# Attention and a mixture of experts on one core: keys and queries loaded head dimension first, the softmax division moved onto x, a column-tiled gate, and longer runs of one tiling

## The chip, the core and the metric

The kernel is one launch on one NeuronCore of a Trainium2 chip. The metric is device time in microseconds (us), the median of several runs; a profiled execution gives the trace that is read here. The engines are named as in the profile: PE (TensorE; PEld is its weight load), DVE (VectorE), ACT (ScalarE), POOL (GpSimd) and SP (SyncE, which here only starts transfers).

## The reference

All data are float32. Attention has 4 batches, 8 heads, 1152 positions and a head dimension of 64; queries are averaged in pairs first, so that 576 are left. Its output becomes x with 2304 rows of 512, which goes through a mixture of 8 experts whose weights P come from eight rounds of row and column scaling (Sinkhorn).

```python
q_pool = q.reshape(B, H, S // 2, 2, D).mean(axis=3)
scores = scale * np.matmul(q_pool, k.transpose(0, 1, 3, 2))
attn = np.exp(scores - scores.max(-1, keepdims=True))
attn = attn / (attn.sum(-1, keepdims=True) + 1e-09)
x = np.matmul(attn, v)                     # to (B*S/2, H*D)
P = np.exp(x @ w_gate - (x @ w_gate).max())
for _ in range(8):
    P /= P.sum(1, keepdims=True) + 1e-09
    P /= P.sum(0, keepdims=True) + 1e-09
    P *= N / E
for e in range(E):
    out += P[:, e:e + 1] * (np.maximum(x @ w1[e], 0.0) @ w2[e])
```

## The kernel before, in words

The program has two stages, attention and then the mixture of experts.

**Attention** goes over 16 pairs of heads (4 batches, 4 pairs). A pair has five units: four full ones, each with 128 queries of both heads, and a mixed one with the last 64 queries of each head. In a unit:

- the scores S are three groups of 384 keys (`qk`, L465). Queries and keys are each split in a high and a low part, so a group takes three products per head. A full unit runs its two heads on two row tiles of the array, 64 rows each; the mixed unit uses the whole array;
- DVE copies S from PSUM to E and keeps the row maximum (`out_max`, L472), ACT takes the exponential in place with its row sum (`expo`, L488), DVE makes the reciprocal of the sum (`rec`, L494 and L495), and ACT or DVE multiplies E by it (`norm`, L503 or L505, 1152 columns at a time);
- PE transposes E, 18 blocks of 128x128 in a full unit and 9 in the mixed one (`tr`, L521), in groups of four that share a PSUM buffer; ACT or DVE copies each group to ET (`tr_out`, L531 or L533);
- PE multiplies ET with the values (`av`, L549), two heads on two column tiles of 64. When a pair's four full units are done, ACT copies the sum to x (`x_out`, L566).

Before a pair starts, its queries and keys are loaded in rows (L378 to L382), POOL adds the two queries of each average (`q_add`, L399 and L402), PE transposes queries and keys (`trans`, L423), ACT writes the high part from PSUM (`hi`, L428) and DVE the low part (`lo`, L436).

The gate's logits are products of 128 rows of x, as weights of the array, with the gate matrix of 8 columns (`gate`, L62). Those of row blocks 0 to 12 run inside attention, the last five at the start of the second stage.

The order of attention is made when the program is built: a planner (`Plan.order`, from L200) keeps for each engine the work that is ready, takes the one of the lowest due time, and places it with a cost in ns. `STICK` is what a PE step gains in due time for having the tiling of the step before; `gap` is the cost of a change of tiling, `WAIT` how long an engine may stay idle for a better step. `CAPS` are the buffers: 2 for S, 3 for transposes, 1 for `av`, 4 for E, 2 for ET. The engines then run their instructions in exactly that order.

**The mixture of experts** (`moe`) is 96 steps of matrix products with split operands: 4032 products of 384 columns (L692 to L694) and 3456 of 512 columns (L729). Here the framework's scheduler sets the order. The Sinkhorn rounds are worked off in small pieces between the steps.

## Time and profile before

| | |
|---|---|
| time, median of 3 runs | 2059.75 us (2058.86 to 2060.17) |
| span of the profiled execution, first to last instruction | 2055.5 us |
| its own time beside the span | not given apart; the median of the runs lies 4.25 us above the span |
| PE busy | 2035.5 us (99%), 13344 instructions |
| PEld busy | 1802.2 us (88%) |
| DVE busy | 1522.8 us (74%) |
| ACT busy | 972.0 us (47%) |
| POOL busy | 336.2 us (16%) |
| granted PE clock, mean of the span | 0.998 |
| DMA | 191952 packets, 135.90 MB, mean 66 GB/s |

A matmul's row gives its start and how long it lay in the array; the next one starts before it ends. What a matmul costs in a stream is therefore read from start to start, not from its duration. A float32 product of x, E or v shows as two matmul records. Attention's products end at 542.4 us, the rest of the gate follows, and the mixture of experts starts at 546.95 us: the first stage is a good quarter of the span.

### The profile page before, as it was taken

Reading aid. Unit: us, or ns where it says so; the run is one execution under the profiler, and the core shown is the slowest. Engines: PE = TensorE matmul, PEld = TensorE weight load, DVE = VectorE, ACT = ScalarE, POOL = GpSimd, SP = SyncE. Lnnn points to the kernel's source line nnn. Section 1 sums busy time; section 2 is a strip of 40 time slices with the busy share of each in tenths; the row PEclk is TensorE's granted clock in tenths of the full one; section 3 lists DMA queues with packets and bytes.
Section 4 is the critical chain, followed back from the end, with each engine's and each line's share of the span. In section 5 each row is a group of like instructions: output and inputs, shape, how many; then the busy total and the mean of one; then the engine's idle time right before and its main releaser. Section 6 shows DMA issues by size and latency. Waiting matters only on the chain.

```text
span 2055.5 us, 33894 instructions
## 1 busy us (share of the span) xinstructions
PE 2035.5 (99%) x13344; PEld 1802.2 (88%) x13344; DVE 1522.8 (74%) x3254; ACT 972.0 (47%) x1617; POOL 336.2 (16%) x424
## 2 busy tenths in 40 slices
PE   8999999999999999999999999999999999999999
PEld 6888888888989999999989999999989999999998
DVE  6787878877698676776776776767776777777764
ACT  6888887888643333233344333333333333333331
POOL 1000011100001112112231211121122112112210
PEclk9999999999999999999999999999999999999999
DMA  5212121210122222222231221222213222222211
GB/s 137 59 48 71 53 54 46 61 47 13 32 82 84 61 83 62 62 73 72 62 103 58 77 70 54 82 62 62 77 47 113 72 65 69 72 59 75 70 54 41
DMA packets 191952, 135.90 MB, mean 66 GB/s; under 512 B 44080, under 2 KB 160816, under 8 KB 191792
## 3 DMA queue, kind: packets, MB, share of 16 engines
q1 hardware_dynamic: 189456, 133.15, 22.3%
q8 instruction: 104, 1.70, 0.4%
q10 hardware_dynamic: 2336, 0.59, 0.1%
q14 instruction: 56, 0.46, 0.1%
HBM read 128.99 MB, written 4.72 MB: 65 GB/s over the span
## 4 chain that ended last, share of the span: by engine, by line
PE 94%; ACT 3%; DVE 2%; DMA 1%; issue 0%; POOL 0%; SPq 0%; ACTq 0%; DVEq 0%
PE pso L729 38%; PE psh L692 11%; PE psh L694 11%; PE psh L693 11%; PE av L549 7%; PE tr L521 7%; PE S L465 6%; PE tr L423 2%; ACT E L488 1%; ACT E L503 1%; ACT ET L531 1%; PE tr L62 1%; DVE xcl L95 0%; DMA qr<-in_q_dram 0%; DVE E L472 0%
## 5 line engine op out<-in xcount | busy, mean ns | idle before, releaser
L701 ACT ACTIVATE hh<-c 128x384 fp32r<-128x384 f32 x384 | 199.9, 521 | 676.0 <-DVE c L712 675.8
L729 PE MATMUL pso<-w2h,hl 128*128 128x512 f32 x1152 | 453.8, 394 | 0.4 <-DVE hl L702 0.4
L692 PE MATMUL psh<-xch,w1h 128*128 128x384 f32 x1344 | 453.0, 337 | 0.7 <-ACT p L707 0.7
L694 PE MATMUL psh<-xch,w1l 128*128 128x384 f32 x1344 | 453.1, 337 | 0.0
L729 PE MATMUL pso<-w2l,hh 128*128 128x512 f32 x1152 | 452.9, 393 | 0.0
L693 PE MATMUL psh<-xcl,w1h 128*128 128x384 f32 x1344 | 451.8, 336 | 0.0
L729 PE MATMUL pso<-w2h,hh 128*128 128x512 f32 x1152 | 447.8, 389 | 0.0
L739 DVE SCALAR_TENSOR_TENSOR x<-pso,PR,x 128x512 f32<-128x512 f32 x264 | 197.4, 748 | 195.6 <-PE pso L729 195.3
L692 PEld LDWEIGHTS psh<-xch,w1h 128*128 128x128 f32 x1344 | 253.0, 188 | 12.7 <-ACT p L707 1.7
L693 PEld LDWEIGHTS psh<-xcl,w1h 128*128 128x128 f32 x1344 | 252.7, 188 | 11.0
L129 POOL TENSOR_TENSOR w1t<-w1s 128x256 f32<-128x256 f32 x88 | 80.9, 920 | 1087.5 <-DMA w1s<-in_moe_w_dram 638.2
L729 PEld LDWEIGHTS pso<-w2h,hl 128*128 128x128 f32 x1152 | 216.0, 188 | 46.2 <-DVE hl L702 0.8
L472 DVE TENSOR_SCALAR_CACHE_REDUCE E<-S 128x384 f32<-128x384 f32 x432 | 222.7, 553 | 43.6 <-PE S L465 41.7
L694 PEld LDWEIGHTS psh<-xch,w1l 128*128 128x128 f32 x1344 | 252.7, 188 | 0.1
L729 PEld LDWEIGHTS pso<-w2l,hh 128*128 128x128 f32 x1152 | 216.1, 188 | 40.0
L729 PEld LDWEIGHTS pso<-w2h,hh 128*128 128x128 f32 x1152 | 216.5, 188 | 38.7
L702 DVE SCALAR_TENSOR_TENSOR hl<-c,hh 128x384 fp32r<-128x384 f32 x384 | 225.2, 587 | 12.2 <-ACT hh L701 0.4
L712 DVE TENSOR_TENSOR c<-psh,u 128x384 f32<-128x384 f32 x288 | 151.2, 552 | 54.4 <-PE psh L694 53.3
L488 ACT ACTIVATE E<-E,st 128x1152 f32<-128x1152 f32 x144 | 179.5, 1252 | 7.0 <-DVE st L478 6.0
L521 PE MATMUL tr<-ident,E 128*128 128x128 f32 x1296 | 172.2, 278 | 4.7 <-ACT ET L531 1.3
L465 PE MATMUL S<-kT,qT 64*128 64x384 f32 (+1 forms) x1296 | 171.7, 362 | 1.3 <-DVE E L472 1.3
L521 PEld LDWEIGHTS tr<-ident,E 128*128 128x128 f32 x1296 | 141.4, 141 | 27.9 <-issue 11.6
(83 smaller groups left out, 2332.5 us busy)
## 6 DMA issues: line engine op xcount, KB each, us to landing
w1s<-in_moe_w_dram SPq DMA_DIRECT2D x192, 256.0 KB, 3.2
w2s<-in_moe_w_dram SPq DMA_DIRECT2D x96, 512.0 KB, 3.6
vt<-in_v_dram SPq DMA_DIRECT2D x16, 576.0 KB, 4.1
kr<-in_k_dram SPq DMA_DIRECT2D x30, 288.0 KB, 4.4
qr<-in_q_dram SPq DMA_DIRECT2D x32, 256.0 KB, 4.3
out_dram<-x SPq DMA_DIRECT2D x18, 256.0 KB, 2.1
qr<-in_q_dram SPq DMA_DIRECT2D x32, 32.0 KB, 4.0
kr<-in_k_dram ACTq DMA_DIRECT2D x2, 288.0 KB, 5.5
```

The source lines that it names most:

```text
L465: nc.tensor.matmul(ps[:, h, :PK], D["qT", p][rows, x, t * P:(t + 1) * P], D["kT", p][rows, y, j * PK:(j + 1) * PK], start=(i == 0), stop=( ...
L472: nc.vector.tensor_scalar(out=D["E", m][:, h, j * PK:(j + 1) * PK], in0=D["sc", m, j][:, h, :PK], scalar1=1.0, scalar2=None, op0=ALU.mult, ...
L488: nc.scalar.activation(out=x, in_=x, func=ACTF.Exp, bias=D["st", m][:, h, 3:4], accum_out=D["rs", p][:, t, h:h + 1])
L521: nc.tensor.transpose(ps[:, i * P:(i + 1) * P], x[:, c * P:(c + 1) * P], ident)
L692: nc.tensor.matmul(ps, hi[:, a, c, :], xch[:, b, c, :], start=(c == 0), stop=False)
L693: nc.tensor.matmul(ps, hi[:, a, c, :], xcl[:, b, c, :], start=False, stop=False)
L694: nc.tensor.matmul(ps, lo[:, a, c, :], xch[:, b, c, :], start=False, stop=(c == 1))
L701: nc.scalar.activation(out=hh[:, fh, ts], in_=src, func=ACTF.Relu)
L702: nc.vector.scalar_tensor_tensor(out=hl[:, fh, ts], in0=src, scalar=0.0, in1=hh[:, fh, ts].bitcast(F32), op0=ALU.max, op1=ALU.subtract)
L712: nc.vector.tensor_tensor(out=y, in0=ps, in1=t, op=ALU.add)
L729: nc.tensor.matmul(ps, u[:, fh, ms], w[:, fh, :], start=(n == 0), stop=(n == 11))
L739: nc.vector.scalar_tensor_tensor(out=a, in0=ps, scalar=PR[:, m, e:e + 1], in1=a, op0=ALU.mult, op1=ALU.add)
```

## The change: what it does

1. **Inputs are laid out before the launch.** A new function `laid_out` reorders the arrays in memory: queries and keys with the head dimension first, values and expert weights so that one transfer loads a tile with long rows per partition. It does no arithmetic. The gate matrix is padded from 8 to 32 columns with zeros.
2. **No input transposes.** `trans` is gone. ACT writes the high part of queries and keys straight from the loaded tile (`q_hi`, `k_hi`), and POOL the low part (`q_lo`, `k_lo`; DVE for the first pair). The factor 0.0625 moves from the queries into `out_max`.
3. **Division on x.** `norm` is gone; the transposes take E right after the exponential. The row sums of a pair's nine heads-by-units lie in one tile; one `rec` per pair adds 1e-9 and inverts. Four small transfers write the 1152 reciprocals to DRAM (`spread_out`), two read them back spread over 64 partitions each (`spread_in`), and POOL multiplies x by them (`x_scale`). What reads x (the gate, the blocks of x for the second stage) now waits for `x_scale`.
4. **Column-tiled gate.** The gate matrix, 32 columns wide, is the weight; x streams 384 columns through, four column tiles at a time; an ACT copy, three transposes and a DVE copy put the logits in place. The last six row blocks follow in the second stage (`last_gate`), after its first step, and the Sinkhorn rounds start there.
5. **The planner's numbers.** `STICK` 0.7 becomes 6.0, `WAIT` 700 becomes 300, the cost of a change of tiling 110 or 60 becomes 195 or 145, `TR0` 12 becomes 14, and the mixed unit's scores count as the same tiling as transposes.

```diff
-        wg = const.tile([P, ND, E], F32, name="wg")
+        wg = const.tile([P, ND, 32], F32, name="wg")
...
-def gate(nc, ps, x, wg, m):
-
-    g, i = divmod(m, MT)
-    for c in range(ND):
-        nc.tensor.matmul(ps, x[:, g, c, i * P:(i + 1) * P], wg[:, c, :], start=(c == 0), stop=(c == ND - 1))
...
+def gate(nc, ps, x, wg, c, chunks, w, t0):
+
+    for j in chunks:
+        g, u = divmod(t0 + j * w, TG)
+        nc.tensor.matmul(ps[32 * j:32 * j + 32, :w], wg[:, c, :], x[:, g, c, u:u + w], start=(c == 0), stop=(c == ND - 1))
...
         t = self.raw1[k] = self.stage.tile([P, 2, ND, P], F32, name="w1s", tag="w1s")
-        for h in range(2):
-            f0 = h * F // 2 + i * P
-            self.nc.sync.dma_start(out=t[:, h], in_=self.w1[e, :, f0:f0 + P].rearrange("(c p) f -> p c f", p=P))
+        self.nc.sync.dma_start(out=t, in_=self.w1[k % (E * FQ)].rearrange("p (h c f) -> p h c f", h=2, c=ND))
...
-    WAIT = 700
+    WAIT = 300
...
-                        gap = 110 if "R2" in (mode, o["mode"]) else 60
+                        gap = 195 if o["mode"] == "R" else 145
...
-TR0 = 12.0
-STICK = 0.7
-CAPS = dict(kr=2, qr=2, vt=2, qa=2, kT=2, qT=2, S=2, tr=3, av=1, E=4, ET=2, st=4, rs=2, avs=2)
-UNIT, MIXED = 5.0, 3.2
+TR0 = 14.0
+STICK = 6.0
+CAPS = dict(kr=2, qr=2, vt=2, qa=2, kT=2, qT=2, S=2, tr=3, av=1, E=4, ET=2, st=4, rs=2, RB=2, lg=1)
+UNIT, MIXED = 6.0, 3.0
...
-        @op("SP", 1800, T - 16, w=[("raw", p)], new=[(("kr", p), "kr"), (("qr", p), "qr")], lat=2500)
-        def load():
-            kr = D["kr", p] = sbt([P, NC, 2, HD], F32, "kr")
-            qr = D["qr", p] = sbt([P, 2 * QT + 1, 2, HD], F32, "qr")
...
+        @op("SP", 1200, T - 16, w=[("q", p)], new=[(("qr", p), "qr")], lat=2500)
+        def load_q():
+            qr = D["qr", p] = sbt([P, 2, Q], F32, "qr")
+            nc.sync.dma_start(out=qr, in_=q[p])
...
-                    nc.tensor.transpose(ps[:, j * P:(j + 1) * P], x, ident)
...
-                nc.scalar.activation(out=D[tag, p][:, 0, c0 * P:(c0 + n) * P], in_=D["ps", p, i][:, :n * P],
-                                     func=ACTF.Copy, scale=0.0625 if what == "q" else 1.0)
...
-                nc.vector.scalar_tensor_tensor(out=t[:, 1, cs], in0=ps, scalar=0.0625 if what == "q" else 1.0,
-                                               in1=t[:, 0, cs].bitcast(F32), op0=ALU.mult, op1=ALU.subtract)
...
+            def q_hi(cs=cs):
+                nc.scalar.activation(out=qT()[:, 0, cs], in_=D["qa", p][:, cs], func=ACTF.Copy)
+
+            @op(ae, cost(ae, n, two=True), T + 5 + 4 * i, r=[("qh", p, i)], w=[("qT", p, i)], use=[("qa", p), ("qT", p)])
+            def q_lo(cs=cs):
+                t = D["qT", p]
+                eng_of[ae].tensor_tensor(out=t[:, 1, cs], in0=D["qa", p][:, cs], in1=t[:, 0, cs].bitcast(F32), op=ALU.subtract)
...
+            def k_hi(cs=cs):
+                nc.scalar.activation(out=kT()[:, 0, cs], in_=D["kr", p][:, cs], func=ACTF.Copy)
+
+            @op(ae, cost(ae, W, two=True), T + 7 + 0.5 * j, r=[("kh", p, j)], w=[("kT", p, j)], use=[("kr", p), ("kT", p)])
+            def k_lo(cs=cs):
+                t = D["kT", p]
+                eng_of[ae].tensor_tensor(out=t[:, 1, cs], in0=D["kr", p][:, cs], in1=t[:, 0, cs].bitcast(F32), op=ALU.subtract)
...
-                    nc.vector.tensor_scalar(out=D["E", m][:, h, j * PK:(j + 1) * PK], in0=D["sc", m, j][:, h, :PK], scalar1=1.0,
+                    nc.vector.tensor_scalar(out=D["E", m][:, h, j * PK:(j + 1) * PK], in0=D["sc", m, j][:, h, :PK], scalar1=0.0625,
...
-        @op("DVE", 260, T + 5.6 + 1.3 * (nt - 1), r=[("X", m, h) for h in heads], w=[("r", m)], use=[("rs", p)])
-        def rec():
-            y = D["rs", p][:, t, :nt]
-            nc.vector.tensor_scalar(out=y, in0=y, scalar1=1e-9, scalar2=None, op0=ALU.add)
-            nc.vector.reciprocal(y, y)
-
-        for h in heads:
-            @op(("DVE", "ACT"), [870, 1053], T + 5.8 + 1.3 * (nt - 1) + 0.1 * h, r=[("r", m)], w=[("E", m, h)], use=[("rs", p), ("E", m)])
-            def norm(eng, h=h):
-                y = D["E", m][:, h]
-                z = D["rs", p][:, t, h:h + 1]
-                if eng == "ACT":
-                    nc.scalar.activation(out=y, in_=y, func=ACTF.Copy, scale=z)
-                else:
-                    nc.vector.tensor_scalar(out=y, in0=y, scalar1=z, scalar2=None, op0=ALU.mult)
...
-            es = [("E", m, h) for h in sorted({c // NC for c in cs})]
+            es = [("X", m, h) for h in sorted({c // NC for c in cs})]
...
+        if mixed:
+            @op("DVE", 260, T + 8, r=[("X", p * (QT + 1) + i, h) for i in range(QT + 1) for h in (range(2) if i < QT else (0,))],
+                w=[("r", p)], use=[("rs", p)])
+            def rec():
+                y = D["rs", p]
+                nc.vector.tensor_scalar(out=y, in0=y, scalar1=1e-9, scalar2=None, op0=ALU.add)
+                nc.vector.reciprocal(y, y)
+
+            @op("SP", 1200, T + 8.2, r=[("r", p)], w=[("rd", p)], use=[("rs", p)], lat=2500)
+            def spread_out():
+                s, y = D["rd", p] = dr.tile([2, Q], F32, name="rd", tag="rd", bufs=2), D["rs", p]
+                for h in range(2):
+                    nc.sync.dma_start(out=s[h, :QM].rearrange("(t p) -> p t", p=P), in_=y[:, h * QT:(h + 1) * QT])
+                    nc.sync.dma_start(out=s[h:h + 1, QM:].rearrange("o p -> p o"), in_=y[64 * h:64 * h + 64, 2 * QT:])
+
+            @op("SP", 1200, T + 8.3, r=[("rd", p)], w=[("RB", p)], new=[(("RB", p), "RB")], lat=2500)
+            def spread_in():
+                R = D["RB", p] = sbt([P, Q], F32, "RB")
+                s = D["rd", p][0]
+                for h in range(2):
+                    nc.sync.dma_start(out=R[64 * h:64 * h + 64], in_=s[h:h + 1].to_broadcast([64, Q]))
+
+            @op("Pool", cost("Pool", Q, two=True), T + 20, r=[("RB", p), ("xu", p, False), ("xu", p, True)], w=[("x", p)],
+                use=[("RB", p)])
+            def x_scale():
+                for i, g, u, w in spans(b * Q, Q):
+                    y = xx[:, g, hp, u:u + w]
+                    nc.gpsimd.tensor_tensor(out=y, in0=y, in1=D["RB", p][:, i:i + w], op=ALU.mult)
...
+        for c in range(ND):
+            @op("PE", 2 * 335, T + 0.1 * c, mode="G", r=[("wg",)] + [("x", p) for p in range(3 * NPAIR)],
+                w=[("gl",)], new=[(("gl",), "tr")] if c == 0 else [], use=[("gl",)] if c else [])
+            def gate_mm(c=c):
+                if c == 0:
+                    D["gl"] = pst([P, 512], "tr")
+                gate(nc, D["gl"], xx, wg, c, range(GC), TH, 0)
...
+        def last_gate():
+            psl = ps2.tile([P, D], F32, name="psl", tag="ps2")
+            for c in range(ND):
+                gate(nc, psl, x, wg, c, range(3), W0, M0 * P)
+            lg = gs.tile([P, W0], F32, name="lg", tag="lg", bufs=1)
+            nc.scalar.activation(out=lg[:96], in_=psl[:96, :W0], func=ACTF.Copy)
+            pst = ps2.tile([P, D], F32, name="pst", tag="ps2")
+            for i in range(2):
+                nc.tensor.transpose(pst[:, i * 96:(i + 1) * 96], lg[:96, i * P:(i + 1) * P], ident[:96, :96])
+            nc.vector.tensor_copy(PR[:, M0:].rearrange("p (j i) e -> p j i e", i=2),
+                                  pst[:, :192].rearrange("p (i j e) -> p j i e", i=2, e=32)[:, :, :, :E])
...
-        fill = sinkhorn()
+        fill = iter(())
...
+            if k == 0:
+                last_gate()
+                fill = sinkhorn()
...
+    q = inputs["q"].reshape(NPAIRS, 2, Q, 2, HD).transpose(0, 1, 4, 3, 2).reshape(NPAIRS, P, 2, Q)
+    k = inputs["k"].reshape(NPAIRS, 2, S, HD).transpose(0, 1, 3, 2).reshape(NPAIRS, P, S)
+    v = inputs["v"].reshape(NPAIRS, 2, NC, P, HD).transpose(0, 3, 1, 2, 4).reshape(NPAIRS, P, 2 * NC * HD)
```

On PE, while the second pair is worked on, the stretch of the kernel before from one run of E's transposes (`tr<-ident,E`) over scores (S), products with the values (av) and transposes of queries and keys (`tr<-ident,qa`, `tr<-ident,kr`) reads:

```order
L521 MATMUL tr<-ident,E 128x128 x18
L465 MATMUL S<-kT,qT 128x384 x12
L423 MATMUL tr<-ident,qa_76 128x128 x4
L549 MATMUL av<-ET,vt 64x128 x18
L465 MATMUL S<-kT,qT 128x384 x6
L521 MATMUL tr<-ident,E 128x128 x9
L423 MATMUL tr<-ident,qa_76 128x128
L465 MATMUL S<-kT,qT 128x384 x12
L549 MATMUL av<-ET,vt 64x64 x12
L521 MATMUL tr<-ident,E 128x128 x12
L465 MATMUL S<-kT,qT 128x384 x6
L549 MATMUL av<-ET,vt 64x64 x6
```

In the changed kernel a stretch of the same engine, of the same length, reads:

```order
L472 MATMUL S<-kT,qT 128x384 x12
L540 MATMUL av<-ET,vt 64x128 x18
L472 MATMUL S<-kT,qT 128x384 x12
L511 MATMUL tr<-ident,E 128x128 x9
L472 MATMUL S<-kT,qT 128x384 x12
L540 MATMUL av<-ET,vt 64x64 x18
L511 MATMUL tr<-ident,E 128x128 x18
L472 MATMUL S<-kT,qT 128x384 x12
L540 MATMUL av<-ET,vt 64x128 x18
L472 MATMUL S<-kT,qT 128x384 x12
L511 MATMUL tr<-ident,E 128x128 x18
L472 MATMUL S<-kT,qT 128x384 x6
```

The transposes of queries and keys are gone, the scores come in runs of 12 and the transposes in runs of 18 or 9. Over the whole of attention the order holds 365 changes between the three tilings (whole array, row tiles, column tiles) before, 129 of them into row tiles; now there are 225, of them 94 into row tiles.

On SP, whose transfers start in this order, rd is the DRAM buffer of the reciprocals, RB their spread form, and kr, qr and vt the keys, queries and values of later pairs; the first rows are those of the first pair's reciprocals:

```order
L380 DMA qr<-in_q_dram 128x1152 x2
L565 DMA rd<-rs 128x4x1
L566 DMA rd<-rs 64x1
L565 DMA rd<-rs 128x4x1
L566 DMA rd<-rs 64x1
L573 DMA RB<-rd 64x576 x2
L389 DMA kr<-in_k_dram 128x1152
L380 DMA qr<-in_q_dram 128x1152
L394 DMA vt<-in_v_dram 128x1152
```

Keys of the fifth pair, queries of the seventh and values of the third now stand behind the two legs of the first pair's reciprocals; before, SP held loads alone here.

On POOL, the steps around the same pair's multiplication of x:

```order
L580 TENSOR_TENSOR x<-x,RB 128x576
L432 TENSOR_TENSOR qT<-qa_79,qT 128x512
L445 TENSOR_TENSOR kT<-kr,kT 128x1152
L432 TENSOR_TENSOR qT<-qa_79,qT 128x128
L411 TENSOR_TENSOR qa_79<-qr 128x512
L418 TENSOR_TENSOR qa_79<-qr 64x64 x2
L580 TENSOR_TENSOR x<-x,RB 128x576
```

POOL's row of low parts (L432, L445) is new, and the multiplication (L580) stands in one queue with them.

## Rows read from the trace of the kernel before

**Rows 1.** Windows: stretch, length, busy us of PE, PEld, DVE, ACT, POOL, clock, DMA, GB/s

```profile
71.65:103.69 32.04, 31.77 (x358) 26.54 (x357) 25.58 (x88) 27.45 (x45) 1.91 (x3) 1.00 0.23 57
547.00:2055.00 1508.00, 1503.56 (x7489) 1355.55 (x7488) 1097.38 (x1833) 526.30 (x895) 291.56 (x363) 1.00 0.23 70
```

**Rows 2.** PE's timeline over one pair: start us, us, engine, line, operation, tile, count

```profile
71.65 2.43 PE L521 MATMUL tr<-ident,E 128*128 128x128 f32 x18
74.02 1.32 PE L465 MATMUL S<-kT,qT 64*128 64x384 f32 x12
75.27 2.19 PE L549 MATMUL av<-ET,vt 128*64 128x128 f32 x36
77.38 0.79 PE L465 MATMUL S<-kT,qT 64*128 64x384 f32 x6
78.11 2.27 PE L521 MATMUL tr<-ident,E 128*128 128x128 f32 x18
80.31 1.31 PE L465 MATMUL S<-kT,qT 64*128 64x384 f32 x12
81.55 0.66 PE L423 MATMUL tr<-ident,qa 128*128 128x128 f32 x4
82.14 2.19 PE L549 MATMUL av<-ET,vt 128*64 128x128 f32 x36
...
88.67 1.53 PE L521 MATMUL tr<-ident,E 128*128 128x128 f32 x12
90.13 0.79 PE L465 MATMUL S<-kT,qT 64*128 64x384 f32 x6
...
102.53 1.31 PE L465 MATMUL S<-kT,qT 128*128 128x384 f32 x6
103.69 1.47 PE L521 MATMUL tr<-ident,E 128*128 128x128 f32 x12
```

**Rows 3.** groups by line: busy us, mean ns of one, idle before and its releaser

```profile
L423 PE MATMUL tr<-ident,kr 128*128 128x128 f32 x144 | 26.6, 298 | 0.7 <-ACT ET L531 0.3
...
L423 PE MATMUL tr<-ident,qa 128*128 128x128 f32 x80 | 15.5, 292 | 6.8 <-ACT ET L531 2.1 <-POOL qa L399 2.0 <-DVE qa L399 1.9
...
L62 PE MATMUL tr<-wg,x 128*128 128x8 f32 x104 | 13.2, 253 | 0.0
```

**Rows 4.** PE's timeline at the start of the program

```profile
6.86 0.65 PE L423 MATMUL tr<-ident,qa 128*128 128x128 f32 x4 [1.88 <-DVE qa L399]
...
10.57 1.11 PE L465 MATMUL S<-kT,qT 64*128 64x384 f32 x6
...
22.70 1.10 PE L521 MATMUL tr<-ident,E 128*128 128x128 f32 x8 [1.08 <-ACT E L503]
```

**Rows 5.** groups by line: the multiplications of E on ACT and DVE

```profile
L503 ACT ACTIVATE E<-E,rs 128x1152 f32<-128x1152 f32 x79 | 99.2, 1256 | 34.0 <-DVE rs L495 33.6 <-ACT ET L531 0.4
...
L505 DVE TENSOR_SCALAR E<-E,rs 128x1152 f32<-128x1152 f32 x65 | 53.9, 831 | 0.7
```

**Rows 6.** PE's timeline where attention ends

```profile
541.15 1.38 PE L549 MATMUL av<-ET,vt 128*64 128x64 f32 x36
542.46 4.63 PE L62 MATMUL psl<-wg,x 128*128 128x8 f32 x40
546.95 0.47 PE L692 MATMUL psh<-xch,w1h 128*128 128x384 f32 x1
```

**Rows 7.** timeline of all engines, POOL beside DVE, at 297 and at 334 us

```profile
297.64 1.27 POOL L399 TENSOR_TENSOR qa<-qr 128x512 f32<-128x512 f32 x1 [18.15 <-PE tr L521]
...
297.97 0.69 DVE L533 COPY ET<-tr 128x512 f32<-128x512 f32 x1
...
334.42 1.86 POOL L88 TENSOR_TENSOR xt<-x,xt 128x768 f32<-128x768 f32 x1 [33.84 <-DVE rs L494]
...
335.05 1.84 DVE L505 TENSOR_SCALAR E<-E,rs 128x1152 f32<-128x1152 f32 x1
```

**Rows 8.** transfers: issuing queue, count, KB each, median us to landing

```profile
vt<-in_v_dram SPq DMA_DIRECT2D x16, 576.0 KB, 4.1
```

More of the change, by code (lines that the diff above doesn't have):

```diff
@@ new lines, in pair_ops @@
+        for j in range(parts):
+            cs = slice(j * W, (j + 1) * W)
+            @op("ACT", cost("ACT", W), T + 5 + 0.5 * j, r=[("k", p, j)] + ([("kh", p, 0)] if j else []), w=[("kh", p, j)], new=[] if j else [(("kT", p), "kT")],
+                use=[("kr", p)] + ([("kT", p)] if j else []))
+            def k_hi(cs=cs):
[4 more added lines that the diff above has]
+                eng_of[ae].tensor_tensor(out=t[:, 1, cs], in0=D["kr", p][:, cs], in1=t[:, 0, cs].bitcast(F32), op=ALU.subtract)
@@ L539, in unit_ops @@
         for j in range(3):
-            @op("PE", 3 * (4 * w / 2.4 + 20), T + TR0 + 2.6 + 0.7 * j, mode="F", r=[("v", p)] + [("ET", m, g) for g in range(-(-nb // 4))],
+            @op("PE", 12 * (29.5 if mixed else 54.5), T + TR0 + 2.6 + 0.7 * j, mode="C",
+                r=[("v", p)] + [("ET", m, g) for g in range(-(-nb // 4))],
                 w=[("av", p, mixed)], new=[(("av", p, mixed), "av")] if new_av and j == 0 else [],
@@ L554, in unit_ops @@
             F = T + TR0 + 4.8
[L555 to L556 removed]
             o = b * Q + (QM if mixed else 0)
[L560 removed]
+            @op("ACT", cost("ACT", n, True), F, r=[("av", p, mixed)], w=[("xu", p, mixed)], use=[("av", p, mixed)])
             def x_out():
[L562 to L565 removed]
+                for i, g, u, w in spans(o, n):
@@ L631, in attention, with moe @@
         pool.release()
-def moe(tc, out, x, xch, xcl, wg, PR, blocks, wt):
+def moe(tc, out, x, xch, xcl, ident, wg, PR, blocks, wt):
     nc = tc.nc
@@ L718, in second @@
             g, e = ks[0] // (FQ * E), ks[0] // FQ % E
+            if half == FQ // 2:
+                for _ in fill:
+                    pass
             m = g * MT + i
```

168 lines of the change are left out of this document (79 added, 89 removed).

## Prediction, made before the changed kernel ran

> **What bounds the kernel now.** I read the windows first, since they give busy time and clock of both stages; then PE's timeline, start to start, inside attention; then the groups by line for what the change takes away; last the start and the end of attention, and the rows where POOL and DVE meet.
>
> The second stage is at PE's pace: from 547 to 2055 us PE is busy for 1503.6 of 1508.0 us at the full clock [rows 1]. The change adds a little gate work to it and reorders nothing else on PE, so its 1508.5 us stand. What is to be had lies in attention.
>
> There one pair of heads takes 32.04 us, from one run of 18 transposes to the same run a pair later, and PE shows 31.77 us busy, DVE 25.58, ACT 27.45 [rows 1]. A busy PE is not yet a working PE, so I take the pace from starts [rows 2]. Scores on row tiles: 12 take 1.24 us (80.31 to 81.55), 6 take 0.73, so 0.085 us each, and 0.22 us that each run pays whatever its length. Transposes: 12 take 1.46 us (88.67 to 90.13), 4 take 0.59 (81.55 to 82.14), so 0.109 each and 0.155 per run. Products with the values: 36 records take 2.11 us (75.27 to 77.38); with 0.15 for the run, 0.0545 a record. Scores of the mixed unit: 6 in 1.16 us (102.53 to 103.69), 0.174 each and 0.12. So a change of tiling costs about 0.22 us into row tiles and 0.155 us into either of the others.
>
> With these the pair adds up: 72 x 0.085 + 9 x 0.174 + 95 x 0.109 (81 transposes of E, 14 of inputs) + 144 x 0.0545 + 36 half-width records at about 0.03 = 27.0 us of work; 23 changes of tiling (8 into row tiles) 4.1 us; 31.1 of 32.04. About 0.95 us a pair is left for waits, and they show where 18 transposes need five groups and there are three PSUM buffers: the run at 71.65 took 2.37 us where 18 x 0.109 + 0.155 is 2.12, the one at 78.11 took 2.20. PE is the bound, with 3% of waits; ACT and DVE stand at 86% and 80%.
>
> The Trainium skill (Perfetto Trace Analysis, Identifying the Most-Contended Engine) says that matmul busy time does not tell how near PE is to its limit and points to the weight loads' busy share. By that, the pair has 26.54 of 32.04 us, 83% [rows 1], and work taken off PE would partly turn into bubbles. The trace does not agree: the sum above, from starts, leaves 3%. By the skill's share the saving below would shrink by a sixth, some 10 us, and stay inside the range.
>
> **The change, part by part.**
>
> Input transposes: 144 + 80 = 224 [rows 3] at 0.109 us, -24.4 us. All of it is on PE's path. Their feeding steps (ACT's high part from PSUM, DVE's low part) go to ACT and POOL from SBUF; on ACT that is about the same work, DVE loses it.
>
> Changes of tiling: 365 before and 225 after by the order; 35 of the difference go into row tiles. 35 x 0.22 + 105 x 0.155 = -24.0 us. If a change cost less in the new neighbourhoods (scores straight to values, for one), the nearest row is the 0.12 of the mixed scores: 140 x 0.12 = 16.8.
>
> Multiplying E: 79 on ACT at 1256 ns and 65 on DVE at 831 ns [rows 5] vanish, 153 us of two engines that are not the bound. They go to nothing by themselves. What they give is a shorter way from exponential to transposes and 6.2 us of ACT and 3.4 of DVE a pair less in front of the copies that the transposes wait for. Against this stand more runs of 18. I keep most of the waits: 0.8 us a pair instead of 0.95, -3 us; bounds 0 (-15) and one more full PSUM copy (0.69 us, [rows 7]) waited for in every run of 18, 64 of them, +44.
>
> Gate inside attention: 104 records before, at 0.112 us (4.49 us for 40, [rows 6]), 11.6 us. Now 16 products of 384 columns; 128 columns on half the array cost 0.109 a product with two abreast, so 0.218 alone, 0.654 for 384; four abreast, four rounds, 2.6 us, and three transposes 0.33. -8.7 us; if the tiles did not run abreast, 10.5 us and no gain.
>
> Start: scores begin at 10.57 us and E's transposes at 22.70 [rows 4]. Now transposes and PSUM copies fall out before the scores (6.86 to 10.57 held 14 transposes) and the multiplication between exponential and transposes, some 1.3 to 1.8 us. Beyond the transposes already counted I take -3 us; bounds -7 and +3 (keys come in long rows now, and three loads share the first microseconds).
>
> End: the last 40 gate records took 4.49 us [rows 6], and under them ACT and DVE cut the first weights. Now 7 products stand there, three rounds of 0.436 us, and then PE may wait for the cut; I take 2.0 to 3 us in place of 4.49. Five more products, two transposes and two changes come later in the stage, 0.9 + 0.2 + 0.4. Together -1 us; bounds -3 and +3.
>
> The spreading of the reciprocals: six transfers a pair on SP and a multiplication on POOL. POOL does 512 elements of two inputs in 1.27 us [rows 7], 2.5 ns an element. A pair now gives it the queries' sum (about 1.9 us), the low parts (1.6 and 2.9) and the multiplication (1.4), near 8 us of 29: not a bound. Behind the six transfers on SP stand keys, queries and values of later pairs; tightest are the values of the next pair but one, wanted when that pair's products begin, a whole pair (29 us) after the multiplication's own pair is done with its buffer. A load lands in 4.1 us [rows 8], the two legs, at the same figure, in 8.2 and their issue below 6: some 18 of 29 us. I cost it at nothing. The gate and the blocks of x stand half a pair or more behind the multiplication they wait for.
>
> Sum: -24.4 - 24.0 - 3 - 8.7 - 3 - 1 = -64 us. On the execution's own span of 2055.5 that is 1991.5; the median of the runs shown lies 4.25 above the span, so 1996 us. As a check, a pair comes to 25.5 us of work, 14 changes of tiling (2.5 us) and 0.8 of waits, 28.8 instead of 32.04.
>
> **The rivals.**
>
> *Fewer waits.* PE waited because copies queue behind work that is now gone; with ACT and DVE at some 70% the waits of transposes vanish and the start gives its whole bound: 13 + 4 us less, 1979 to 1983. For it: before, no score and no product with the values shows a wait, only transposes. Against it: three PSUM buffers remain.
>
> *Long runs wait for their copies.* Every run of 18 waits for one PSUM copy more, +44 us less the usual 3: about 2038. For it: the 0.25 us at 71.65. Against it: the run at 78.11 paid 0.09 with both copying engines fuller than they will be.
>
> *POOL holds DVE.* A multiplication of E on DVE took 1.84 us beside POOL instead of 0.83, while a copy from PSUM beside POOL took its usual 0.69 [rows 5, 7]. The DVE steps left in attention read PSUM, so I expect nothing. If copies were held all the same, POOL works 28% of the time, and 42 of some 150 copies would lose about 1 us; half of that on PE's path gives 2017. The Trainium skill (SBUF: State Buffer, Who interferes with whom) says that DVE's copies in a two-port mode, or steps with two SBUF inputs, and POOL block each other for a whole instruction; of the multiplication the trace agrees, of the PSUM copies it shows no such block.
>
> *The spread starves the loads (slower).* Writing 1152 separate 4-byte values a pair may take far longer than a load. From 25 us for both legs on, the values come late, and PE pays every further us in 14 pairs. At 30 us that is 70 us, more than the whole saving: 2066. For it: no row shows such small pieces. Against it: everything on record lands in about 4 us.
>
> **How the numbers follow.** Forecast 0.62, own range 1984 to 2010; fewer waits 0.17; long runs 0.12; POOL holds DVE 0.05; starved loads 0.04. The range for 8 in 10 takes in the second case and the near end of the others: 1978 to 2022. About 0.2%, 4 us, is what a measurement can tell from no change; all cases but the last lie far below it: faster 0.96, within 0.01, slower 0.03.
>
> **What would show it.** In the new trace the input transposes are absent, a run of 12 scores still takes 1.24 us to the next start, 18 transposes 2.1 to 2.4; a pair takes 28 to 29.5 us; the 16 gate products take about 2.8 us; the first product of the second stage starts near 484 us, and the stage behind it lasts 1507 to 1512 us. I am wrong if a pair stays above 30.5 us, if PE shows waits for S or for keys, or if the second stage grows.

## The result, and the profile after

The changed kernel takes 2002.07 us (median of four runs, 1999.31 to 2004.46) beside 2059.96 us of the kernel before on the same chip: ratio 0.9718, 95% interval 0.9705 to 0.9731, 57.9 us less. The forecast was 1996 us. It missed by 6 us, and the experiments show that this is a gain of 7 to 8 us more than forecast and a loss of 13 us that was forecast at nothing.

First the windows, as in [rows 1]: two successive pairs of heads in attention and the second stage (stretch, length, busy us of PE, PEld, DVE, ACT, POOL, clock, DMA, GB/s).

```profile
92.25:120.81 28.56, 28.56 (x344) 25.12 (x342) 20.18 (x70) 20.78 (x37) 7.62 (x8) 1.00 0.24 75
120.81:151.34 30.53, 28.88 (x344) 25.09 (x343) 20.08 (x70) 20.91 (x37) 7.63 (x8) 1.00 0.23 70
488.00:1997.00 1509.00, 1504.01 (x7500) 1354.26 (x7500) 1105.14 (x1837) 526.70 (x897) 297.67 (x364) 1.00 0.21 70
```

The second stage has its length of before (1509 us). The first pair takes 28.56 us, where 28.8 was forecast and 32.04 was measured before. The second does the same work and takes 30.53: PE shows 1.65 us in which it isn't busy, where the pair of before had 0.27. Counted from the mixed unit's first scores, most pairs take 28.9 to 30.5 us, four take 28.5 to 28.6, and one, with the gate's products in it, 33.4.

PE's timeline shows where the 2 us go (columns as in [rows 2], in brackets the idle time ahead and what ended it).

```profile
120.81 1.32 PE L472 MATMUL S<-kT,qT 64*128 64x384 f32 x12
122.07 2.33 PE L511 MATMUL tr<-ident,E 128*128 128x128 f32 x18
124.33 1.32 PE L472 MATMUL S<-kT,qT 64*128 64x384 f32 x12
125.58 2.19 PE L540 MATMUL av<-ET,vt 128*64 128x128 f32 x36
127.69 1.31 PE L472 MATMUL S<-kT,qT 64*128 64x384 f32 x12
128.94 1.20 PE L511 MATMUL tr<-ident,E 128*128 128x128 f32 x9
131.62 0.79 PE L472 MATMUL S<-kT,qT 64*128 64x384 f32 x6 [1.49 <-DVE E L479]
132.58 0.79 PE L472 MATMUL S<-kT,qT 64*128 64x384 f32 x6 [0.17 <-DVE E L479]
133.30 1.27 PE L540 MATMUL av<-ET,vt 128*64 128x64 f32 x36
```

Twelve scores still take 1.25 us to the next start and 18 transposes 2.26: the pace is that of before. But the nine transposes at 128.94 are followed by scores only at 131.62, and those wait for DVE. PE's waits over attention, by releaser (us in total, times, longest), give the sum:

```profile
PE S L472 <- DVE E L479: 7.8, 20, 1.5
```

Is DVE too slow? Its timeline, ACT's and SP's of the same moment:

```profile
127.27 0.08 DVE L479 DVE_READ_ACCUMULATOR E<-S 128x1 f32 x1
130.53 0.56 DVE L479 TENSOR_SCALAR_CACHE_REDUCE E<-S 128x384 f32<-128x384 f32 x1 [3.17 <-PE tr L511]
```

```profile
128.93 0.57 ACT L551 ACTIVATE x<-av 128x512 f32<-128x512 f32 x1
130.73 1.25 ACT L521 ACTIVATE ET<-tr 128x512 f32<-128x512 f32 x3 [1.22 <-PE tr L511]
```

```profile
119.51 0.38 SPq L565 DMA_DIRECT2D rd<-rs  x1
119.94 0.51 SPq L566 DMA_DIRECT2D rd<-rs  x1
120.49 0.58 SPq L565 DMA_DIRECT2D rd<-rs  x1
121.12 0.51 SPq L566 DMA_DIRECT2D rd<-rs  x1
130.81 1.34 SPq L573 DMA_DIRECT2D RB<-rd  x2
```

DVE stands idle from 127.35 to 130.53, though PE had gone on from the scores that it wants at 128.94; ACT is idle too. The trace has no semaphore event of PE between 127.79 and 130.50. (A semaphore is the counter by which one engine tells another that a step is done; the trace holds an event for each of these signals.) PE has ended the scores for DVE by 129.01 and the first transposes for ACT by 129.59, but both are told only from 130.50 on, and PE then waits for DVE. The signal comes together with the landing of the reciprocals: SP can start the reading leg (line 573) at 130.81, 9.7 us after it issued the last writing one, where loads land in 4.1 us [rows 8].

I counted the matmuls whose semaphore event comes over 0.25 us after their end: 41 in attention after, up to 2.47 us late, in groups that recur once in most pairs; none in the kernel before. From here on they are called late signals. They are late for those who wait: ACT or DVE starts some 0.02 us after most of these events. Of 15 signals of ACT, 12 of DVE and 3 of POOL the trace of the changed kernel has no event at all; in the kernel before none is missing. A missing event doesn't mean a late signal. DVE's maximum (line 485) ends at 38.72, the next event of DVE on record is at 43.04, and yet ACT's exponential, which waits for that maximum, starts at 38.76:

```profile
38.56 0.16 DVE L485 TENSOR_REDUCE st<-st 128x2 f32<-128x6 f32 x1
38.76 1.26 ACT L495 ACTIVATE E<-E,st 128x1152 f32<-128x1152 f32 x1 [1.67 <-issue]
```

So only PE's signals are shown to be late. Where the profile gives "issue" or "remote" as the end of a wait, it has found no event that fits, and in such a stretch that can be a missing or a late one.

The rest answers the rows of before. Groups by line, beside [rows 3]: the transposes of keys and queries have gone, and the gate stands on column tiles.

```profile
L511 PE MATMUL tr<-ident,E 128*128 128x128 f32 x1296 | 169.5, 279 | 0.2
...
L72 PE MATMUL tr<-x,wg 128*32 128x384 f32 x32 | 2.8, 489 | 0.0
```

PE's timeline at the start [rows 4] and where attention ends [rows 6]:

```profile
7.13 2.75 PE L472 MATMUL S<-kT,qT 64*128 64x384 f32 x12 [1.79 <-ACT kT L440]
...
14.71 2.57 PE L511 MATMUL tr<-ident,E 128*128 128x128 f32 x18
...
485.18 1.48 PE L72 MATMUL psl<-x,wg 128*32 128x256 f32 x14
487.93 0.44 PE L726 MATMUL psh<-xch,w1h 128*128 128x384 f32 x1 [1.26 <-ACT w1h L149]
```

E's first transposes start 8.0 us earlier than before. At the end, 2.75 us stand in place of 4.49, 1.26 of them a wait for the first weights' cut.

### The profile page after: what moved, and what is told of

The parts are those of the page before. It is cut to its first block, busy times and chain, and to the rows that moved or that the text cites. A ratio compares the mean times of both kernels' runs of the same rounds, so it can differ in the third digit from the quotient of the medians.

```text
span 1997.5 us, 32950 instructions
## 1 busy us (share of the span) xinstructions
PE 1978.0 (99%) x13037; PEld 1763.3 (88%) x13037; DVE 1440.9 (72%) x2982; ACT 865.7 (43%) x1502; POOL 429.6 (22%) x493
## 4 chain that ended last, share of the span: by engine, by line
PE 74%; DVE 1%; DMA 0%; POOL 0%; issue 0%; ACT 0%; DVEq 0%; ACTq 0%
PE pso L766 39%; PE psh L726 12%; PE psh L728 12%; PE psh L727 12%; DVE xcl L105 0%; DMA w2s<-in_moe_w_dram 0%; POOL xt L98 0%; DVE x L776 0%; DVE hl L736 0%; DVE c L746 0%; DVE w1l L154 0%; DVE w2l L165 0%; PE psl L72 0%; DVE u L746 0%; ACT xch L102 0%
## 5 line engine op out<-in xcount | busy, mean ns | idle before, releaser
L135 POOL TENSOR_TENSOR w1t<-w1s 128x256 f32<-128x256 f32 x88 | 66.6, 757 | 1071.8 <-DMA w1s<-in_moe_w_dram 1033.3
L736 DVE SCALAR_TENSOR_TENSOR hl<-c,hh 128x384 fp32r<-128x384 f32 x384 | 231.8, 605 | 13.0 <-ACT hh L735 1.2
L472 PE MATMUL S<-kT,qT 64*128 64x384 f32 (+1 forms) x1296 | 167.1, 360 | 9.8 <-DVE E L479 7.8
```

Of the source, the lines that this page charges most:

```text
L472: nc.tensor.matmul(ps[:, h, :PK], D["qT", p][rows, x, t * P:(t + 1) * P], D["kT", p][rows, y, j * PK:(j + 1) * PK], start=(i == 0), stop=( ...
L736: nc.vector.scalar_tensor_tensor(out=hl[:, fh, ts], in0=src, scalar=0.0, in1=hh[:, fh, ts].bitcast(F32), op0=ALU.max, op1=ALU.subtract)
```

## The experiments

All times are medians; every ratio is to the kernel before, run on the same chip in the same rounds. Differences below 3 us are not read as effects: the changed kernel's own four runs spread over 5 us. In e1_36b, e6_plan36, e7_768 and e9_256b x is multiplied by reciprocals in another order, so their output is not the reference's; they price the way through DRAM. The late signals are those of attention.

| run | us (range) | ratio, 95% interval | late signals of PE |
|---|---|---|---|
| changed kernel | 2002.07 (1999.31 to 2004.46) | 0.9718 [0.9705, 0.9731] | 41 |
| e1_36b | 1988.84 (1988.59 to 1989.37) | 0.9655 [0.9642, 0.9668] | 0 |
| e2_rows | 1996.60 (1995.48 to 1997.93) | 0.9692 [0.9679, 0.9705] | 0 |
| e3_double | 2127.73 (2125.37 to 2131.01) | 1.0329 [1.0314, 1.0345] | 100 |
| e4_plan | 2044.03 (2041.33 to 2045.42) | 0.9920 [0.9907, 0.9934] | 62 |
| e5_16b | 1987.90 (1986.78 to 1988.95) | 0.9651 [0.9637, 0.9664] | 3 |
| e6_plan36 | 2004.55 (2004.13 to 2005.85) | 0.9731 [0.9717, 0.9745] | 0 |
| e7_768 | 1991.00 (1989.85 to 1994.81) | 0.9668 [0.9654, 0.9681] | 20 |
| e8_norm | 2003.98 (2003.86 to 2005.02) | 0.9728 [0.9715, 0.9742] | 0 |
| e9_256b | 1987.03 (1985.30 to 1988.29) | 0.9648 [0.9634, 0.9661] | 0 |
| e10_tr14 | 2012.29 (2011.68 to 2013.03) | 0.9771 [0.9758, 0.9784] | 9 |
| e11_wait600 | 1993.14 (1991.64 to 1993.82) | 0.9678 [0.9665, 0.9691] | 9 |
| e12_steps | 2016.57 (2015.01 to 2018.66) | 0.9792 [0.9779, 0.9806] | 52 |

My theory: the writes of 4 bytes hold the signals between the engines while they land. Its rivals: instruction blocks, which are fetched at the same moment of a pair, or too few buffers for E.

**e1_36b: fewer, larger pieces.**

```
-  for h in range(2):
-      dma_start(out=s[h, :QM].rearrange("(t p) -> p t", p=P), in_=y[:, h*QT:(h+1)*QT])
-      dma_start(out=s[h:h+1, QM:].rearrange("o p -> p o"), in_=y[64*h:64*h+64, 2*QT:])
+  dma_start(out=s.rearrange("h (a c) -> (h a) c", c=2*QT+1), in_=y)
```

> The reciprocals of a pair go to DRAM as 128 pieces of 36 bytes in one transfer instead of 1152 pieces of 4 bytes in six (x is then multiplied by reciprocals in another order; everything else stands). Theory (small pieces: while they land, what PE has finished is told to DVE up to 2.5 us late, once per pair): the waits of scores for DVE in attention, 7.8 us in 20 rows, fall below 1 us, a pair takes 28.6 us each time, and the second stage starts 8 to 12 us earlier, near 478: 1990 to 1994 us. Rival 1 (instruction blocks that are fetched once per pair at the same moment): they are still fetched, so 7 to 8 us of waits stay and the time is 2000 to 2004 us. Rival 2 (DVE itself is late with the exponentials because four E tiles are too few): same waits, same time.

1988.84 us, 13.2 less, no late signal, and no event missing. (Of the six transfers of the expectation four write and two read.) PE's wait for DVE over attention falls to 0.4 us, and most pairs take 28.57 to 28.73 us. SP's timeline shows the way through DRAM: 1.6 us from issue to reading leg instead of 9.7.

```profile
118.74 0.33 SPq L564 DMA_DIRECT2D rd<-rs  x1
120.29 1.09 SPq L571 DMA_DIRECT2D RB<-rd  x2
```

PE's order is the same to the row, E has the same four tiles and the instructions are still fetched. Both rivals fall as they were put: blocks and buffers alone don't hold anything. That the writes slow the fetching of the blocks is not excluded by this run.

**e2_rows: PE transposes the reciprocals first, DRAM gets rows of 512 bytes.**

```
+  nc.tensor.transpose(D["rp", p][:2*QT+1, :P], D["rs", p], ident)     # then a copy to rT, on ACT or DVE
-  dma_start(out=s[h, :QM].rearrange("(t p) -> p t", p=P), in_=y[:, h*QT:(h+1)*QT])
+  dma_start(out=s[h, :QM].rearrange("(t p) -> t p", p=P), in_=rT[h*QT:(h+1)*QT])
```

> The reciprocals of a pair are transposed by PE first (one more transpose and one small PSUM copy per pair), so that they go to DRAM as rows of 512 bytes; the output is the reference's. PE pays 14 transposes and 14 more changes of tiling, 14 x (0.109 + 0.155) = 3.7 us. Theory (small pieces): the waits of scores for DVE go, -8 to -12, and +3.7 for the transposes: 1993 to 1998 us. Rival 1 (instruction blocks): waits stay, 2003 to 2008 us. Rival 2 (too few E tiles): as rival 1.

1996.60 us, no late signal: the signals as expected. A pair takes 29.2 us, 0.65 more than without the transpose, where 0.26 was expected: the reciprocals take one of three PSUM buffers, and a run of 19 transposes behind them takes 2.66 us (155.51 to 158.17), 0.4 more than the pace of the prediction gives. That it waits for a copy is likely, but no row shows it.

**e3_double: the same pieces twice.**

```
+  z = dr.tile([2, Q], F32, name="rz", tag="rz", bufs=2)               # nobody reads it
+  for h in range(2): (the two transfers of 4-byte pieces, into z)
```

> The reciprocals are written to DRAM twice per pair, the second time into a place that nobody reads: 2304 pieces of 4 bytes instead of 1152. Theory (small pieces): the writing takes near 20 us instead of 10 and the late tellings last twice as long or come twice per pair; another 8 to 12 us of waits, 2010 to 2014 us. Should the values of a later pair come late behind it on SP's queue, more than that. Rival 1 and 2 (instruction blocks, too few E tiles): 2000 to 2004 us.

2127.73 us: 126 more, where 8 to 12 were expected. In one pair, PE, DVE and ACT, after SP's last writing leg at 113.67:

```profile
121.49 0.80 PE L540 MATMUL av<-ET,vt 128*64 128x64 f32 x19
127.77 1.64 PE L540 MATMUL av<-ET,vt 128*64 128x64 f32 x17 [5.48 <-issue]
```

```profile
120.73 0.16 DVE L485 TENSOR_REDUCE st<-st 128x2 f32<-128x6 f32 x1
128.35 0.56 DVE L479 TENSOR_SCALAR_CACHE_REDUCE E<-S 128x384 f32<-128x384 f32 x1 [7.46 <-remote]
```

```profile
119.88 1.09 ACT L521 ACTIVATE ET<-tr 128x512 f32<-128x512 f32 x2 [0.21 <-issue]
127.49 0.28 ACT L521 ACTIVATE ET<-tr 128x128 f32<-128x128 f32 x1 [6.53 <-remote]
```

```profile
113.67 0.51 SPq L570 DMA_DIRECT2D rd<-rs  x1
128.50 1.11 SPq L577 DMA_DIRECT2D RB<-rd  x2
```

All three engines stand still for 5.5 to 7.5 us, and the stop ends just ahead of the reading leg. ACT and DVE wait for PE: its transposes ended by 120.33 and are told at 127.47, its scores ended at 121.56 and are told by 128.40. ACT's own signals are not held. The event of its copy that ended at 120.96 is missing, but PE's load of weights that waits for it starts at 121.95. PE itself stops at 122.29 in the middle of a run, at an instruction that waits for no semaphore; what stops it no run shows. Instructions are fetched there too: one block of 16384 bytes took 4.3 us, where PE's others in the first 340 us of this trace take 0.9 to 2.3, but it landed at 121.47. In other pairs PE stops because DVE or ACT, which waited for PE, are late themselves. A pair takes 34 to 42 us. Part of that is TensorE's clock. PE was busy for 0.79 of the 6 us of this stop, and for the 3.5 us behind it the granted clock is 0.50 of full speed, the lower of its two levels (1.2 GHz); over the first 600 us its mean is 0.90, where the other runs have 0.98 to 1.00.

```profile
121.50:127.50 6.00, 0.79 (x21) 0.67 (x20) 0.00 (x0) 0.01 (x1) 0.00 (x0) 0.73 0.00 0
127.50:131.00 3.50, 3.20 (x25) 3.04 (x26) 2.44 (x9) 2.85 (x6) 0.00 (x0) 0.50 0.21 14
0.00:600.00 600.00, 501.33 (x5438) 433.29 (x5439) 334.75 (x1143) 338.15 (x599) 132.70 (x129) 0.90 0.22 58
```

**e4_plan: the planner's numbers of before.**

```
-  WAIT = 300; gap = 195 if o["mode"] == "R" else 145; TR0 = 14.0; STICK = 6.0; UNIT, MIXED = 6.0, 3.0
+  WAIT = 700; gap = 110 if "R" in (mode, o["mode"]) else 60; TR0 = 12.0; STICK = 0.7; UNIT, MIXED = 5.0, 3.2
```

> The changed kernel with the planner's six numbers of the kernel before: 322 changes of tiling in attention instead of 225 (32 of the difference into row tiles), the input transposes still gone. By the predicted term (0.22 us into row tiles, 0.155 into the others) the longer runs are worth 32 x 0.22 + 65 x 0.155 = 17.1 us: 2017 to 2021 us, unless the shorter runs also wait less for DVE (then 2010 to 2015). Rival (a change of tiling costs 0.12 or less, or long runs wait for PSUM copies what they save): 2000 to 2012 us, and at nothing or below 2002.

2044.03 us, 42 more than the changed kernel and more than any theory gave. The late signals were the suspicion, 62 of them, up to 4.6 us late. So this run alone prices nothing; e6_plan36 takes the small pieces out.

**e5_16b: the order in DRAM follows the tile, POOL reads with a stride.**

```
-  dma_start(out=s[h, :QM].rearrange("(t p) -> p t", p=P), in_=y[:, h*QT:(h+1)*QT])
+  dma_start(out=s[h, :QM].rearrange("(p t) -> p t", t=QT), in_=y[:, h*QT:(h+1)*QT])
+  R = D["RB", p][:, :QM].rearrange("d (p t) -> d t p", t=QT)          # in1 of POOL's multiplication
```

> The reciprocals go to DRAM in the order in which they lie in a row of the tile (128 pieces of 16 bytes per head, and the last 64 of each head in pieces of 4 bytes: 384 pieces a pair instead of 1152), and POOL's multiplication reads them back with a stride; the output is the reference's and PE does nothing more. Theory (many small pieces hold the signals between the engines): as with 128 pieces, no late signals, pairs of 28.6 us, 1987 to 1992 us. Rival (the price goes with the count: 13.2 us for 1024 pieces a pair fewer): a quarter of it stays, 1991 to 1994 us. Rival (any 4-byte pieces hold them): 1996 us and more.

1987.90 us: the fastest version in which each x gets its own reciprocal, 14.2 us ahead of the changed kernel and 3.5% below the kernel before. Three late signals are left, up to 0.74 us, where none was expected. The way through DRAM now takes 5.5 us here, and POOL's multiplication 1.82 us instead of 1.43, on an engine with room.

```profile
119.39 0.47 SPq L580 DMA_DIRECT2D rd<-rs  x1
124.91 1.11 SPq L587 DMA_DIRECT2D RB<-rd  x2
```

```profile
132.07 1.82 POOL L602 TENSOR_TENSOR x<-x,RB 128x512 f32<-128x512 f32 x2 [8.61 <-ACT x L565]
```

**e6_plan36: the edits of e4_plan and of e1_36b together.**

> The planner's numbers of before together with 128 pieces of 36 bytes (x is multiplied by reciprocals in another order, as in the first run): 322 changes of tiling instead of 225, and nothing that holds signals. If the extra 25 us of the run with those numbers and small pieces were held signals that shorter runs met worse, the term alone is left: 32 x 0.22 + 65 x 0.155 = 17.1 us above 1988.8, so 2004 to 2008 us. Rival (a change of tiling costs about 42 / 97 = 0.43 us, or shorter runs wait for something else): 2025 to 2031 us. Rival (0.12 each): 2000 us.

2004.55 us. Against e1_36b that is 15.7 us for 97 changes of tiling, 0.162 us each (expected 17.1, 0.176 each). But the changes aren't all of it. In pairs without a wait (this run's 20 changes first, then the 14 of e1_36b) the six more cost 0.81 us, 0.14 each:

```profile
201.51:230.91 29.40, 29.40 (x344) 25.07 (x344) 20.68 (x71) 20.62 (x38) 7.80 (x8) 1.00 0.23 73
...
198.14:226.73 28.59, 28.59 (x345) 25.13 (x344) 20.15 (x70) 20.85 (x39) 7.78 (x8) 1.00 0.23 75
```

Two other pairs take 35.0 and 31.4 us. In both a step of DVE with two inputs from SBUF, which takes 0.95 us alone, took 3.2 us beside POOL, and PE then waited 2.5 and 1.8 us for DVE's copies:

```profile
270.13 3.22 DVE L105 TENSOR_TENSOR xcl<-x,xch 128x768 fp32r<-128x768 f32 x1
274.96 0.69 PE L511 MATMUL tr<-ident,E 128*128 128x128 f32 x2 [2.48 <-DVE ET L523]
```

Behind the first of these waits the granted clock is 0.50 from 274.6 to 281.4. The small pieces cost 39.5 us with these shorter runs (e4_plan against this run) and 13.2 with the longer ones: what a held signal costs depends on the order of the work that meets it.

**e7_768: one head in pieces of 4 bytes, one of 16.**

```
+  z = s[h, :QM].rearrange("(p t) -> p t", t=QT) if h else s[h, :QM].rearrange("(t p) -> p t", p=P)
```

> One head's reciprocals in pieces of 4 bytes, the other's in pieces of 16 (its x is multiplied by reciprocals in another order): 768 pieces a pair, between 384 and 1152. With 1152 pieces the held signals cost 13 us, with 2304 some 139, so the price grows faster than the count: I expect 0 to 4 us for 768, 1988 to 1993 us, and signals that are late by less than 0.5 us. Rival (price by the count): 1988.8 + 13.2 x 640 / 1024 = 1997 us.

1991.00 us, as expected, though single signals are up to 1.6 us late. With 128, 384, 768, 1152 and 2304 pieces a pair the times are 1988.8, 1987.9, 1991.0, 2002.1 and 2127.7 us: the price grows much faster than the count. At 768 the time alone can't be told from nothing.

**e8_norm: E multiplied on ACT and DVE again, nothing spread.**

```
+  nc.scalar.activation(out=E, in_=E, func=Copy, scale=rs)   or   nc.vector.tensor_scalar(out=E, in0=E, scalar1=rs, op0=mult)
-  spread_out, spread_in, x_scale
```

> E is multiplied by the reciprocals on ACT and DVE before its transposes, as in the kernel before, and nothing is spread through DRAM; the rest of the change stands. The order has 267 changes of tiling instead of 225 (14 of the difference into row tiles): 14 x 0.22 + 28 x 0.155 = 7.4 us. Theory (the multiplications cost nothing by themselves, about 3 us of waits): 1988.8 + 7.4 + 3 = 1999 us, 1995 to 2004, that is no slower than the change with its spread. Rival (ACT and DVE fuller by 153 us are late with the PSUM copies): 2010 us and more.

2003.98 us, at the upper end of the range. 42 more changes of tiling at 0.14 to 0.162 make 6 to 7 of the 15.1 us against e1_36b; 8 to 9 stay for the multiplications, not 3. PE's waits for steps of DVE and ACT on E and for copies to ET are 8.0 us in attention, where e1_36b has 0.4. About 2 us lie at the start: the first mixed scores begin at 28.49 instead of 26.45. With its small pieces the change's spread was worth 1.9 us, less than can be told; with larger ones it is worth 16.

**e9_256b: 1280 pieces of 256 bytes beside the 128 of 36.**

```
+  z = dr.tile([5, 2, P, 64], F32, name="rz", tag="rz", bufs=2)
+  for a in range(5): dma_start(out=z[a].rearrange("k p c -> p k c"), in_=ident.rearrange("p (k c) -> p k c", c=64))
```

> As the first run (128 pieces of 36 bytes, x multiplied by reciprocals in another order), and beside it, at the same moment of each pair, 1280 pieces of 256 bytes from a constant tile to a place in DRAM that nobody reads, in five transfers. Theory (it is the many writes of a few bytes that hold the signals, not the number of pieces alone: the kernel before moved over 190000 packets and showed no late signal): no late signals, 1987 to 1993 us. Rival (the number of pieces written in one burst decides): like the 1152 pieces of 4 bytes or worse, signals late by 1 to 3 us in every pair, 2002 us or more.

1987.03 us, no late signal, and no event missing. The transfers (count, KB each, median us to landing) land fast:

```profile
rz<-ident SPq DMA_DIRECT2D x80, 64.0 KB, 1.7
...
rd<-rs SPq DMA_DIRECT2D x16, 4.5 KB, 1.6
```

So more pieces than in the changed kernel, and 71 times its bytes, hold nothing. It is many pieces of a few bytes, written to DRAM, that do. No run wrote over a thousand pieces of 16 or 36 bytes, so where between 4 and 256 bytes it ends is open.

**e10_tr14: 14 idle transposes a pair put into e5_16b.**

```
+  idle = 7 if g == 0 and t in (0, 2) else 0
+  for i in range(idle): nc.tensor.transpose(ps[:, :P], x[:, i*P:(i+1)*P], ident)
```

> The kernel with pieces of 16 bytes (1987.9 us) with 14 idle transposes a pair put in front of transposes of E, seven in each of two runs, 224 in all, as many as the change took away. The order has 223 changes of tiling (224 without them). By the predicted term of the removed input transposes: 224 x 0.109 = 24.4 us, 2010 to 2014 us. Rival (PE waits for ACT's and DVE's copies in those runs anyway, so part of it is hidden): 2000 to 2008 us.

2012.29 us, 24.4 above e5_16b, as predicted; the nine late signals are in it too, and the runs can't tell tenths. Pairs without a wait take 30.06 us instead of 28.57, so 0.106 for each of the 14. PE's timeline shows why nothing is hidden: the seven take 0.82 us and the 18 behind them their usual 2.26.

```profile
106.39 0.98 PE L527 MATMUL tr<-ident,E 128*128 128x128 f32 x7
107.21 2.33 PE L529 MATMUL tr<-ident,E 128*128 128x128 f32 x18
109.47 1.31 PE L486 MATMUL S<-kT,qT 64*128 64x384 f32 x12
```

**e11_wait600: still longer runs of transposes in e5_16b (WAIT = 600).**

> The kernel with pieces of 16 bytes with one planner number changed (it waits up to 600 instead of 300 ns for an operation of earlier due time): 209 changes of tiling instead of 224, all 15 fewer out of runs of transposes. By 0.155 to 0.162 us each: 2.3 to 2.4 us less, 1984 to 1987 us. Rival (the longer runs of transposes then wait for their PSUM copies, four groups against three buffers): 1988 us and more.

1993.14 us, 5.2 slower: the rival holds. It isn't the nine late signals: most pairs take 28.99 us where those of e5_16b take 28.57. A run of 27 transposes finds its PSUM buffers not yet copied.

```profile
157.81 1.20 PE L525 MATMUL tr<-ident,E 128*128 128x128 f32 x9
159.21 2.54 PE L525 MATMUL tr<-ident,E 128*128 128x128 f32 x18 [0.20 <-ACT ET L535]
161.68 1.33 PE L486 MATMUL S<-kT,qT 64*128 64x384 f32 x12
```

From 157.81 to 161.68 it takes 3.87 us, where 27 at 0.109 and one change make 3.1.

**e12_steps: all 4-byte pieces, a unit at a time (the reciprocals are then made for each unit too).**

```
+  dma_start(out=s[:, t*P:(t+1)*P].rearrange("h p -> p h"), in_=y[:, t:t+QT+1:QT])     # after each unit
```

> All 1152 pieces of 4 bytes a pair stay, but each unit's reciprocals go out as soon as they are there: four times 256 pieces and once 128, some 6 us apart, instead of all within 2 us; the output is the reference's. The order has 235 changes of tiling (225 with one burst): +1.6 us. Theory (what is outstanding at one time holds the signals): none late, 1988 to 1992 us. Rival (each piece has its price wherever it stands): 2002 to 2005 us.

2016.57 us, worse than both. The pairs that meet no late signal take 29.4 us, 0.85 more than in e1_36b, some 12 us over attention: the trace has 264 changes of tiling, 17 in most pairs instead of 14, not the 235 of the expectation. At 0.14 to 0.162 that is half of it; the other half is open. The other 16 us I put down to the late signals, 52 of them, and to 10.2 us at the lower clock, though at most 256 pieces go out at a time. So my theory that the number outstanding at one time decides is wrong; nearer is that the pieces cost together what they cost in one burst. Here loads stand beside them as well, and packets of 4608 bytes, which take 0.18 us in the median and at most 1.4 in the changed kernel, took up to 8.0 us, 230 of them over 3. Why 256 pieces are enough is open.

## Why the prediction was right, and where it missed

**The bound.** Right. PE's pace from starts explains the new pair (28.57 us in e1_36b, 28.8 forecast), and by e10_tr14 every transpose on PE is paid in full. The weight loads' share, 88% of the pair at 92.25 (25.12 of 28.56), would have left room that isn't there.

**Input transposes.** -24.4 forecast; 24.4 to put as many back, 23.7 by the pairs without a wait.

**Changes of tiling.** 0.14 us each in pairs without a wait and at most 0.162 over the whole of e6_plan36, instead of a mean of 0.176; so the 140 are worth 19 to 23 us, not 24.0. The Trainium skill (TensorEngine Tiling (Array Packing), Key Properties) says that a change of tiling drains TensorE. The runs agree in that each change costs PE time, the 0.14 us.

**Multiplying E.** The prediction said "They go to nothing by themselves", with 3 us for shorter waits. e8_norm gives 8 to 9 us, in waits of PE: the mechanism is right, the term was too small by 5 to 6, of which 2 lie at the start and belong to that term.

**Gate.** 2.8 us forecast for its products in attention, 2.8 measured.

**Start and end.** E's first transposes came 8.0 us earlier; the 14 input transposes there are 1.5 of it, so some 6 in place of 3, inside the bounds. Part of this is TensorE's clock. In the trace of before the granted clock was at its lower level (0.50) from 14.7 to 18.1, behind 3.4 us in which PE was busy for 1.36:

```profile
14.70:18.10 3.40, 3.24 (x19) 2.07 (x15) 2.09 (x8) 0.59 (x2) 0.30 (x2) 0.50 1.11 314
```

The changed kernel's trace has 1.00 throughout its start. By my estimate, half of PE's 3.24 busy us, that is 1.6 us. The end: 2.75 us between 2.0 and 3.

**The spread.** This is the step that failed: "I cost it at nothing". As a load it is free, as argued: from the first issue at 119.51 POOL's multiplication starts at 135.59, 16 us later, below the 18 of the prediction, and the next values are in time. But it costs 13.2 us (e1_36b against the changed kernel) by a way that I had not thought of: while the pieces land, it holds the signals of PE, which has nothing to do with them, and DVE, ACT and then PE itself wait. The rival with the spread had the right suspect ("no row shows such small pieces") with the wrong victim: no load was late.

The Trainium skill (DMA: Bandwidth & Descriptors, Anatomy of one DMA, written there for transfers that GpSimd issues) says that a transfer is told as done only once the memory has confirmed its last byte, and that this can be long for DRAM. The trace agrees: the last packets of 4 bytes are on record before 123 us, 7 ns each, and the reading leg starts at 130.81. PE's own signals wait meanwhile too, until 130.50 here; why, no run shows.

**The sum.** Without held signals the change gives 1988 to 1989 us, 7 to 8 below the forecast: about 3 from the start, 3 from 14 pairs at 28.57 instead of 28.8, the rest not told apart. With 13.2 on top it is 2002. The forecast fell between the two, so its closeness is partly luck: two misses of opposite sign.

**The signs of being wrong.** One of those that the prediction names came up: PE waits for S, 7.8 us in 20 rows. The pair at 120.81 takes 30.53 us, just over the 30.5, but pairs don't stay there. Both go with the small pieces (0.4 us of waits and pairs of 28.57 us in e1_36b), so they point at the spread, not at the bound.

**The rivals.** *Fewer waits* is half true: 1988 with large pieces, not 1979 to 1983. Pairs without a late signal show no wait, but a run of 18 still takes 2.26 us, 0.14 over the pace. *Long runs wait for their copies* is wrong for runs of 18 and right for 27 (e11_wait600). *POOL holds DVE*: POOL has 7.6 us a pair, as forecast, and the pair at 92.25 has no wait at all. But not all of DVE's steps in attention read PSUM, as the prediction has it: line 105 reads SBUF twice, and beside POOL it took 3.2 us instead of 0.95 in e6_plan36 and 2.0 once in the changed kernel, there without a wait of PE. *The spread starves the loads*: not with 1152 pieces.

## What to carry to other kernels

When several engines stand idle at once and each names another, or nothing, as what it waits for, check when the signals of each went out, and don't take a missing event for a late one; then look at what the DMA queues wrote a few microseconds earlier; a scatter of 4-byte values to DRAM can cost more on the engines than on its queue, and laying the values down in the order of the tile and reading them back with a stride removed nearly all of it here. A cost that no row shows belongs in the sum as a range, not as a zero: here it was 13 of 58 us. Price a parameter of the order only once such disturbances are out: the same six numbers were worth 42 us with small pieces and 15.7 without, and even of these 4.3 are waits in two pairs.
